# Start of a fused attention and feed-forward kernel: second weight chunk loaded behind the first tokens, one cast shared by two engines, one copy moved ahead, one more warming matmul

## The chip, the cores and the metric

The kernel runs on one core of a Trainium2 chip. The metric is the device time of one execution in microseconds (us). A core has five engines that run their own instruction streams in order and wait for each other by semaphores: TensorE (PE in the profile, with its weight loads as PEld), VectorE (DVE), ScalarE (ACT), GpSimd (POOL) and SyncE (SP). SP and ACT here also issue transfers between the chip's memory and the core's own memory.

## The reference, cut to what matters

Two branches read the same tokens x, 2048 of them with 512 channels, in 32-bit floats. Branch A is a sliding, dilated local attention with 32 heads of 16 channels and a window of 8 keys at a distance of 2. Branch B is a gated feed-forward layer with 1792 hidden channels. A sigmoid gate per token mixes both.

```
qkv = x @ wqkv                      # 512 -> 1536, split into q, k, v of 32 heads
logits = q . k[pos - 2*w], w = 0..7, scaled; softmax over w
a = (sum over w of attn * v[pos - 2*w]) @ wo
b = (gelu(x @ w_gate) * (x @ w_up)) @ w_down
g = sigmoid((x * gate_w).sum(-1))
out = g * a + (1 - g) * b
```

## The kernel before, in words

Every product of 32-bit matrices is made of three matmuls. An operand is split into a high part (rounded to the matmul's own format, `hi`, a copy on ACT) and a low part (the rest, `lo`, a subtraction on DVE). Then high times high, low times high and high times low are summed in a bank of the accumulator memory. The tokens come in two halves of 1024, and each half in 8 tiles of 128 tokens. The larger products are moreover done with a scheme of seven block products instead of eight, so that sums of blocks (s1, s2, t1 and so on) are formed first.

The change is only in the first microseconds, in `start()` (lines 867 to 1082), which makes the queries and keys of the first half of the tokens. What it holds:

- The weights of this stage are four blocks of 1024 columns, b11, b21, b12 and b22, each with two chunks k=0 and k=1 of 512 columns. The tokens are blocks a11, a12, a21 and a22, each with two chunks k=0 and k=1, of 128 channels by 512 tokens.
- Lines 72 to 80 run `WARM` matmuls on zeros, so that TensorE is at work while the first data is on its way.
- Lines 884 to 895 issue the loads. The two chunks of b11 (256 KB each) are issued by ACT (`nc.scalar`). SP issues the first 128 tokens of a11 k=0 (64 KB), its other 384 tokens (192 KB), a11 k=1 (256 KB), b21 (512 KB), then a12 and the rest.
- Lines 915 to 922 split the first operands: `tokens(0, P)` casts and subtracts the first 128 tokens on DVE, `hi("b11", 0)` is on ACT, `lo("b11", 0)` on DVE, then the other tokens, and the k=1 chunks of a11 and b11.
- Lines 923 to 933 are the matmuls of k=0: three for the first tile of 128 tokens, `FILLERS` (2) small ones on zeros, then nine for the other three tiles (t=1 to 3). Line 935 runs the twelve of k=1, tile by tile, three for each. That ends the first sums, U[0] to U[3].
- Lines 936 to 938 split b21 and a12 (the third chunk of weights and its tokens). Lines 939 to 941 copy the four sums U to four other banks V_ on ACT, and line 942 adds a12 times b21 to the copies, 24 matmuls, six for each tile: three with k=0, three with k=1.

What sets the order: `row`, `act` and `mms` (lines 775 to 789) are wrappers of DVE, ACT and PE that chain each instruction to the one written before it on that engine. So on these engines the order in time is the order in the program, and an instruction that waits holds back all that is written after it. In the profile all these instructions have line 787, so they are told apart by their tiles: `g<-prod` is a part of b11 or b21 (raw weights lie in `prod`), `A<-raw` a part of the tokens, `acc` the banks U, `p` the banks V_, `p<-acc` the copies of the sums.

After `start()` come the feed-forward products of the first half with the attention's vector work between them, then the same for the second half, and the output product.

Of the kernel before, what the change touches and what calls it, by code (L numbers as in the profile page):

```python
# [12 lines left out]
AF = mybir.ActivationFunctionType  # L13
# [16 lines left out]
UC = 128  # L30
UH = UC // DH
NU = D // UC
WARM = 16
FILLERS = 2
ASK = (0.3, 0.3, 0.3, 0.6, 1.0, 1.2, 1.2)
BEHIND = 150
# [2 lines left out]
BT = 4  # L39
# [5 lines left out]
QW = 2 * P  # L45
# [3 lines left out]
def tile_gated_mix(ctx: ExitStack, tc: tile.TileContext, xt, wqkv, wff, wo, out):  # L49
    nc = tc.nc  # L50
# [10 lines left out]
    def tl(tag, dt=F32):  # L61
        return pool.tile([P, COLS.get(tag, 512)], dt, name=tag, bufs=BUFS[tag])
# [5 lines left out]
    def bank(tag):  # L68
        return psum.tile([P, 512], F32, name=tag, bufs=BUFS.get(tag, 1))
# [6 lines left out]
    idle = [bank("p") for _ in range(4)]  # L76
    for i in range(WARM):
        c = i // 4 % 2 * QW
# [69 lines left out]
    def shift(par, queue, i, j):  # L148
        k = KQ["a"][:, :2 * NP - 1]
        if not i:  # L150
            nc.gpsimd.memset(k[:1, :NP - 1], 0.0)
        for a, b in (1, P - 15), (P - 15, P):
            queue.dma_start(k[a:b, i:j], k[a - 1:b - 1, NP + i:NP + j])
# [300 lines left out]
    def product(ps, a, w, start):  # L454
        for kc in range(2):
            ah, al = XOP[a, kc]
            wh, wl = (x[:, kc * P:(kc + 1) * P] for x in w)
            for n, (w_, a_) in enumerate(((wh, ah), (wh, al), (wl, ah))):
                LAST[:] = [nc.tensor.matmul(ps, w_, a_, start=(start and kc == 0 and n == 0),  # L459
                                            stop=(kc == 1 and n == 2), skip_group_check=True)]  # L460
# [328 lines left out]
    row, act, mms = Row(nc.vector), Row(nc.scalar), Row(nc.tensor)  # L789
# [5 lines left out]
    SRC, OP_, Q2, RAWS = {}, {}, {}, {}  # L795
# [15 lines left out]
    def hi(n, k):  # L811
        return act.activation(OP_[n, k][0], SRC[n, k], AF.Copy)

    def lo(n, k):
        h, l = OP_[n, k]
        row.tensor_tensor(l, SRC[n, k], h.bitcast(F32), op=OP.subtract)

    def both(f, *ns):
        for n in ns:
            for k in range(2):  # L820
                f(n, k)

    def sub(o, a, b):
        row.tensor_tensor(o, a, b, op=OP.subtract)
# [4 lines left out]
    def block(ps, a, w, first, kcs=(0, 1), ask=0.0):  # L829
        for t in range(BT):  # L830
            for kc in kcs:
                ah, al = OP_[a, kc]
                wh, wl = OP_[w, kc]
                for n, (a_, w_) in enumerate(((ah, wh), (al, wh), (ah, wl))):
                    mm(ps[t], t, a_, w_, first and kc == 0 and n == 0, kc == 1 and n == 2)
            if ask:
                pull(ask)

    def out_of(o, ps):
        act.activation(o, ps, AF.Copy)  # L840
# [26 lines left out]
    def start():  # L867
        room_x(0)
        wr = stage("prod", (2, W, UC))
        b11, b21 = wr[:, :1024], wr[:, 1024:]  # L870
# [6 lines left out]
        def load_w(dst, hh, half, cols=slice(0, 1024), queue=nc.sync):  # L877
            queue.dma_start(dst[:, cols], wqkv[hh, half, :, cols])

        def load_x(blk, kc, a=0, n=512):  # L880
            o = (2 * blk + kc // 2) * 512 + a
            nc.sync.dma_start(XR[kc % 2][:, o:o + n], xt[blk, :, kc, a:a + n])

        for k in range(2):
            load_w(b11, 0, 0, slice(k * 512, k * 512 + 512), nc.scalar)
        load_x(0, 0, 0, P)
        load_x(0, 0, P, 512 - P)
        load_x(0, 1)
        load_w(b21, 0, 1)
        load_x(0, 2)  # L890
# [16 lines left out]
        U = [bank(f"acc{t}") for t in range(BT)]  # L907

        def tokens(a, b):
            h, l = (x[:, a:b] for x in OP_["a11", 0])  # L910
            raw = SRC["a11", 0][:, a:b]
            row.tensor_copy(h, raw)
            row.tensor_tensor(l, raw, h.bitcast(F32), op=OP.subtract)

        tokens(0, P)
        hi("b11", 0)
        lo("b11", 0)
        tokens(P, 512)
        hi("a11", 1)
        hi("b11", 1)  # L920
        lo("a11", 1)
        lo("b11", 1)
        (xh, xl), (wh, wl) = OP_["a11", 0], OP_["b11", 0]
        mm(U[0], 0, xh, wh, True)
        mm(U[0], 0, xl, wh)
# [7 lines left out]
                mm(U[t], t, a, w)  # L933

        block(U, "a11", "b11", False, (1,))
        for n, k in (("b21", 0), ("a12", 0), ("b21", 1), ("a12", 1)):
            hi(n, k)
            lo(n, k)
        V_ = [bank("p") for _ in range(BT)]
        for t in range(BT):  # L940
            act.activation(V_[t], U[t], AF.Copy)
        block(V_, "a12", "b21", False)

        def put(jj, ps):
            take_first(0, ps, jj, lambda o, i: act.activation(o, i, AF.Copy))
# [22 lines left out]
        for k in range(2):  # L968
            row.tensor_tensor(s12[k], q[k][2], q[k][3], op=OP.add)
        put(0, V_[0])  # L970
        both(hi, "s1")
        put(1, V_[1])
        sub(b11, b12, b11)
        for k in range(2):
            hi("t1", k)
            lo("s1", k)
            lo("t1", k)
        put(2, V_[2])
        put(3, V_[3])
        shift(0, nc.sync, 0, BT - 1)  # L980
# [49 lines left out]
        for kc in range(KC):  # L1030
            t = tl("d", F32R)
# [89 lines left out]
    def kq_second():  # L1121
# [94 lines left out]
        done.add((1, 2))  # L1216

    start()
    gc = pool.tile([P, 2, NP], F32, name="gc")
    en = pool.tile([P, NP], F32, name="en")  # L1220
# [51 lines left out]
```

## Time and profile before

| | us |
|---|---|
| median of 3 runs | 597.06 (596.82 to 597.29) |
| the profiled execution's own time | 596.87 |
| its span, first to last instruction | 594.8 |
| PE busy | 590.1 |
| DVE busy | 529.4 |
| ACT busy | 389.9 |

A timeline row reads: start in us from the beginning of the span, duration, engine, line, operation, tiles written and read, shape, count, and in brackets the idle time of the engine before it with what ended it. A matmul's record is longer than its distance from the next, because matmuls are pipelined; the distance between starts is what counts. A row of the table by stretch has the stretch, its length, the busy time of PE, PEld, DVE, ACT and POOL, and then the granted clock, the share of busy DMA engines and their rate. An execution's time stands above its span by what lies around it, 2.07 us here.

### The profile page before, as it was taken

Reading aid. Unit: us, or ns where it says so; the run is one execution under the profiler, and the core shown is the slowest. Engines: PE = TensorE matmul, PEld = TensorE weight load, DVE = VectorE, ACT = ScalarE, POOL = GpSimd, SP = SyncE. Lnnn points to the kernel's source line nnn. Section 1 sums busy time; section 2 is a strip of 40 time slices with the busy share of each in tenths; the row PEclk is TensorE's granted clock in tenths of the full one; section 3 lists DMA queues with packets and bytes.
Section 4 is the critical chain, followed back from the end, with each engine's and each line's share of the span. In section 5 each row is a group of like instructions: output and inputs, shape, how many; then the busy total and the mean of one; then the engine's idle time right before and its main releaser. Section 6 shows DMA issues by size and latency. Waiting matters only on the chain.

```text
span 594.8 us, 8195 instructions
## 1 busy us (share of the span) xinstructions
PE 590.1 (99%) x2778; PEld 494.1 (83%) x2778; DVE 529.4 (89%) x618; ACT 389.9 (66%) x668; POOL 89.2 (15%) x121
## 2 busy tenths in 40 slices
PE   9999999999999999999999999999999999999997
PEld 6889988888888888888889988888888888888886
DVE  5997979899998999799989888999999989799952
ACT  5845556787679767788773375677668666885532
POOL 0501001111111111102035000111111111101300
PEclk9999999999999999999999999999999999999999
DMA  8789897988989898998589948795967796737924
GB/s 316 264 250 244 238 306 217 261 245 200 273 215 300 225 261 230 240 312 304 192 249 306 276 137 264 168 244 145 272 157 226 183 269 157 220 109 193 143 57 155
DMA packets 80449, 134.18 MB, mean 226 GB/s; under 512 B 8092, under 2 KB 46362, under 8 KB 80152
## 3 DMA queue, kind: packets, MB, share of 16 engines
q1 hardware_dynamic: 62890, 97.67, 49.9%
q0 software_dynamic: 12576, 32.97, 28.4%
q10 hardware_dynamic: 4942, 3.01, 1.6%
q8 instruction: 22, 0.36, 0.3%
q14 instruction: 19, 0.16, 0.1%
HBM read 68.30 MB, written 38.86 MB: 180 GB/s over the span
## 4 chain that ended last, share of the span: by engine, by line
PE 99%; DVE 0%; ACT 0%; issue 0%
PE p L459 45%; PE acc L502 13%; PE p L502 13%; PE acc L130 8%; PE acc L787 8%; PE p L720 5%; PE p L787 5%; PE acc L720 2%; PE p L79 1%; DVE r L766 0%; ACT rt L768 0%; DVE zero L73 0%
## 5 line engine op out<-in xcount | busy, mean ns | idle before, releaser
L459 PE MATMUL p<-S,g 128*128 128x512 f32 x672 | 166.5, 389 | 0.0
L459 PEld LDWEIGHTS p<-S,g 128*128 128x128 f32 x672 | 125.7, 188 | 25.8
L459 PE MATMUL p<-A,g 128*128 128x512 f32 x504 | 126.7, 390 | 0.0
L459 PEld LDWEIGHTS p<-A,g 128*128 128x128 f32 x504 | 94.3, 188 | 19.6
L417 POOL DMA_DIRECT2D g<-raw x40 | 34.5, 862 | 280.3 <-ACT g L416 208.8
L228 DVE TENSOR_REDUCE lg<-prod 128x128 f32<-128x2048 f32 x32 | 72.9, 2279 | 0.1
L502 PE MATMUL p<-d,hh 128*128 128x512 f32 x224 | 68.5, 389 | 0.0
L502 PE MATMUL acc<-d,hh 128*128 128x512 f32 x224 | 58.1, 389 | 0.0
L287 DVE TENSOR_TENSOR prod<-kq,lg 128x2048 f32<-128x2048 f32 x24 | 54.7, 2279 | 0.9 <-PE p L459 0.5
L421 ACT ACTIVATE g<-raw 128x1024 fp32r<-128x1024 f32 (+1 forms) x40 | 39.5, 991 | 19.0 <-PE p L459 19.0
L502 PEld LDWEIGHTS acc<-d,hh 128*128 128x128 f32 x224 | 42.0, 188 | 8.7
L502 PEld LDWEIGHTS p<-d,hh 128*128 128x128 f32 x224 | 42.0, 188 | 8.7
L416 ACT ACTIVATE g<-raw 128x1024 fp32r<-128x1024 f32 (+1 forms) x40 | 39.5, 987 | 12.0 <-DVE raw L398 4.6
L469 DVE TENSOR_TENSOR c<-p,s 128x512 f32<-128x512 f32 x56 | 37.8, 682 | 6.8 <-PE p L459 6.0
L464 ACT ACTIVATE s<-p 128x512 f32<-128x512 f32 x56 | 33.2, 594 | 15.0 <-PE p L459 13.5
L476 DVE TENSOR_TENSOR hl<-c,hh 128x512 fp32r<-128x512 f32 x56 | 38.1, 680 | 5.5 <-ACT hh L475 5.5
L502 PE MATMUL p<-d,hl 128*128 128x512 f32 x112 | 42.8, 389 | 0.0
L475 ACT ACTIVATE hh<-c 128x512 fp32r<-128x512 f32 x56 | 35.1, 628 | 10.7 <-DVE c L473 10.6
L473 DVE TENSOR_TENSOR c<-c 128x512 f32<-128x512 f32 x56 | 38.2, 682 | 4.3 <-ACT c L570 4.1
L518 ACT ACTIVATE rt<-p 128x512 f32<-128x512 f32 x48 | 28.2, 595 | 20.1 <-PE p L502 20.1
L291 DVE TENSOR_TENSOR prod<-prod 128x1024 f32<-128x1024 f32 x32 | 39.0, 1218 | 0.2
L130 PE MATMUL acc<-d,A 128*128 128x256 f32 (+1 forms) x288 | 37.9, 281 | 0.0
(183 smaller groups left out, 982.0 us busy)
## 6 DMA issues: line engine op xcount, KB each, us to landing
g<-raw POOLq DMA_DIRECT2D x27, 512.0 KB, 6.6
raw<-wff SPq DMA_DIRECT2D x42, 256.0 KB, 3.7
ws<-g SPq DMA_DIRECT2D x14, 768.0 KB, 6.2
g<-ws SPq DMA_DIRECT2D x14, 768.0 KB, 5.4
r<-wff SPq DMA_DIRECT2D x28, 256.0 KB, 4.8
d<-r POOLq DMA_DIRECT2D x24, 256.0 KB, 6.4
g<-raw POOLq DMA_DIRECT2D x13, 384.0 KB, 6.4
os<-tb SPq DMA_DIRECT2D x64, 64.0 KB, 3.8
```

The source lines that it names most:

```text
L130: LAST[:] = [nc.tensor.matmul(ps[:, :cn], a[:, t], w[:, c0:c0 + cn], start=(kc == 0 and n == 0), stop=(kc == KC - 1 and n == 2))]
L228: nc.vector.tensor_reduce(two_of(lg, jj), prod.rearrange("p j w (h d) -> p (j w) h d", d=DH), axis=AX.X, op=OP.add)
L287: paced(nc.vector.tensor_tensor(prod.rearrange("p j w (h d) -> p (j w) h d", d=DH), spans(v, jj).rearrange("p j w (h d) -> p j w h d", d=D ...
L291: nc.vector.tensor_tensor(prod[:, :, :4], prod[:, :, :4], prod[:, :, 4:], op=OP.add)
L416: nc.scalar.activation(lo, raw, AF.Copy, scale=-1.0)
L421: ins = nc.scalar.activation(hi, raw, AF.Copy)
L459: LAST[:] = [nc.tensor.matmul(ps, w_, a_, start=(start and kc == 0 and n == 0), stop=(kc == 1 and n == 2), skip_group_check=True)]
L473: nc.vector.tensor_tensor(ge, ge, up, op=OP.mult)
L476: nc.vector.tensor_tensor(hl_, ge, hh_.bitcast(F32), op=OP.subtract)
L502: ins = nc.tensor.matmul(pp, a[:, ts], w, start=(i == 0 and n == 0 and gr == 0), stop=(i == 1 and n == 2), skip_group_check=True)
L720: ins = nc.tensor.matmul(pa, a, b, start=(first and n == 0), stop=(last and n == 2), skip_group_check=True)
L787: return lambda *args, **kw: self.add(getattr(self.eng, name)(*args, **kw))
```

## The change

The constant `WARM` goes from 16 to 17. The second chunk of b11 is no longer issued by ACT, but by SP, behind the two loads of a11 k=0 and ahead of a11 k=1. The high part of b11 k=0 is made in two halves of 256 columns (`QW`), the first by ACT, the second by DVE ahead of the low part. The k=1 chunk of b11 is split ahead of that of a11, on both engines. The banks V_ are taken earlier, and the copy of U[0] stands in ACT's order ahead of the splits of b21 and a12; the other three copies stay behind them. `out_of` is the same copy on ACT as was written out before.

```diff
-WARM = 16
+WARM = 17
...
-        for k in range(2):
-            load_w(b11, 0, 0, slice(k * 512, k * 512 + 512), nc.scalar)
+        load_w(b11, 0, 0, slice(0, 512), nc.scalar)
         load_x(0, 0, 0, P)
         load_x(0, 0, P, 512 - P)
+        load_w(b11, 0, 0, slice(512, 1024))
         load_x(0, 1)
         load_w(b21, 0, 1)
...
         tokens(0, P)
-        hi("b11", 0)
+        wh, wraw = OP_["b11", 0][0], SRC["b11", 0]
+        act.activation(wh[:, :QW], wraw[:, :QW], AF.Copy)
+        row.tensor_copy(wh[:, QW:], wraw[:, QW:])
         lo("b11", 0)
         tokens(P, 512)
+        hi("b11", 1)
         hi("a11", 1)
-        hi("b11", 1)
+        lo("b11", 1)
         lo("a11", 1)
-        lo("b11", 1)
...
         block(U, "a11", "b11", False, (1,))
-        for n, k in (("b21", 0), ("a12", 0), ("b21", 1), ("a12", 1)):
+        V_ = [bank("p") for _ in range(BT)]
+        for t, (n, k) in enumerate((("b21", 0), ("a12", 0), ("b21", 1), ("a12", 1))):
+            if not t:
+                out_of(V_[t], U[t])
             hi(n, k)
             lo(n, k)
-        V_ = [bank("p") for _ in range(BT)]
-        for t in range(BT):
-            act.activation(V_[t], U[t], AF.Copy)
+        for t in range(1, BT):
+            out_of(V_[t], U[t])
         block(V_, "a12", "b21", False)
```

## The prediction

> **What bounds the kernel now.** I read the page first, its busy line and its chain, and then a table of busy time by stretch, because a mean over 595 us says nothing of the ten microseconds that the change touches.
>
> ```profile
> span 594.8 us, 8195 instructions
> PE 590.1 (99%) x2778; PEld 494.1 (83%) x2778; DVE 529.4 (89%) x618; ACT 389.9 (66%) x668; POOL 89.2 (15%) x121
> PE 99%; DVE 0%; ACT 0%; issue 0%
> ...
> 13.40:40.00 26.60, 26.60 (x119) 22.05 (x118) 24.56 (x37) 19.59 (x40) 8.38 (x16) 1.00 0.82 265
> 40.00:560.00 520.00, 520.00 (x2476) 437.94 (x2475) 480.88 (x548) 351.25 (x596) 78.25 (x98) 1.00 0.83 229
> ```
>
> The chain that ended last is TensorE for 99%, and from 13.40 us to 560 us PE's busy time equals the stretch (first figure the length, second PE). So whatever PE has lost or won when it enters the long stream at about 13.4 us is carried to the end one for one; nothing later absorbs it. The whole question is at what time PE reaches one given matmul there. I take the first matmul of the second token block after the partial sums are copied (V block, t=1), which starts at 13.13. The timeline of PE, first merged and then single instructions from narrow stretches:
>
> ```profile
> 1.07 3.60 PE L79 MATMUL p<-zero 128*128 128x256 bf16 x16 [1.07 <-DVE zero L73]
> 4.67 1.65 PE L787 MATMUL acc<-g,A 128*128 128x512 f32 x3
> 5.26 0.63 PE L787 MATMUL acc<-g,A 128*128 128x512 f32 x1
> 5.69 0.63 PE L787 MATMUL acc<-g,A 128*128 128x512 f32 x1
> 6.12 0.44 PE L787 MATMUL acc<-zero 128*128 128x128 bf16 x2
> 6.49 5.44 PE L787 MATMUL acc<-g,A 128*128 128x512 f32 x21
> 8.71 0.63 PE L787 MATMUL acc<-g,A 128*128 128x512 f32 x2
> 9.37 0.50 PE L787 MATMUL acc<-g,A 128*128 128x512 f32 x1
> 9.71 0.40 PE L787 MATMUL acc<-g,A 128*128 128x512 f32 x1
> 11.77 5.60 PE L787 MATMUL p<-g,A 128*128 128x512 f32 x24
> 12.68 0.39 PE L787 MATMUL p<-g,A 128*128 128x512 f32 x1
> 12.90 0.39 PE L787 MATMUL p<-g,A 128*128 128x512 f32 x1
> 13.13 0.39 PE L787 MATMUL p<-g,A 128*128 128x512 f32 x1
> ```
>
> Read the starts. 24 matmuls of the V block take 5.60, so one follows another at (5.60 - 0.39) / 23 = 0.227 us. Before about 6.6 the clock is half of that: 5.26 to 5.69 is 0.43 for the same 512 columns, and 5.26 - 4.67 = 0.59 shows 0.16 more for a first weight load that nothing covered. The nine of k=0 run from 6.49 to 8.71. In k=1 the second starts at 8.71 + 0.63 - 0.39 = 8.95, the third only at 9.37, and the fourth 0.34 after that, 0.11 over the rhythm: a restart after a wait costs 0.11. From there it is dense to 13.13 and beyond. The two engines that feed it, ACT first, then DVE:
>
> ```profile
> 3.99 0.63 ACT L787 ACTIVATE g<-prod 128x512 fp32r<-128x512 f32 x1 [1.02 <-DMA prod<-wqkv]
> 7.36 0.63 ACT L787 ACTIVATE A<-raw 128x512 fp32r<-128x512 f32 x1 [2.74 <-DMA raw<-xt]
> 7.90 0.62 ACT L787 ACTIVATE g<-prod 128x512 fp32r<-128x512 f32 x1
> 8.61 0.63 ACT L787 ACTIVATE g<-prod 128x512 fp32r<-128x512 f32 x1
> 9.28 0.63 ACT L787 ACTIVATE A<-raw 128x512 fp32r<-128x512 f32 x1
> 9.82 0.62 ACT L787 ACTIVATE g<-prod 128x512 fp32r<-128x512 f32 x1
> 10.34 0.62 ACT L787 ACTIVATE A<-raw 128x512 fp32r<-128x512 f32 x1
> 10.86 2.04 ACT L787 ACTIVATE p<-acc 128x512 f32<-128x512 f32 x4
> 13.33 0.39 ACT L787 ACTIVATE kq<-p 128x256 f32<-128x256 f32 x1 [0.43 <-PE p L787]
> ```
>
> ```profile
> 3.72 0.23 DVE L787 CAST A<-raw 128x128 fp32r<-128x128 f32 x1 [2.63 <-DMA raw<-xt]
> 3.98 0.29 DVE L787 TENSOR_TENSOR A<-raw,A 128x128 fp32r<-128x128 f32 x1
> 4.65 0.69 DVE L787 TENSOR_TENSOR g<-prod,g 128x512 fp32r<-128x512 f32 x1 [0.38 <-ACT g L787]
> 6.08 0.36 DVE L787 CAST A<-raw 128x384 fp32r<-128x384 f32 x1 [0.73 <-DMA raw<-xt]
> 8.02 0.69 DVE L787 TENSOR_TENSOR A<-raw,A 128x512 fp32r<-128x512 f32 x1 [0.99 <-ACT A L787]
> 8.63 0.68 DVE L787 TENSOR_TENSOR g<-prod,g 128x512 fp32r<-128x512 f32 x1
> 9.27 0.69 DVE L787 TENSOR_TENSOR g<-prod,g 128x512 fp32r<-128x512 f32 x1
> 9.95 0.69 DVE L787 TENSOR_TENSOR A<-raw,A 128x512 fp32r<-128x512 f32 x1
> 10.55 0.69 DVE L787 TENSOR_TENSOR g<-prod,g 128x512 fp32r<-128x512 f32 x1
> 11.16 0.69 DVE L787 TENSOR_TENSOR A<-raw,A 128x512 fp32r<-128x512 f32 x1
> ```
>
> On ACT: 3.99 is the high part of b11 k=0; 7.36 that of the tokens a11 k=1, at the moment when its data lands; 7.90 of b11 k=1; 8.61 to 10.34 the four of b21 and a12 (the third chunk), and 10.86 the four copies of the sums. On DVE the low parts follow: 8.02 a11, 8.63 b11, then four from 9.27 to 11.16 + 0.69 = 11.85. The third matmul of k=1 waits at 9.37 for b11's low part (8.63 + 0.68 = 9.31).
>
> **Part by part.** *One more warming matmul.* The 16 stand 0.21 apart ((3.60 - 0.42) / 15, a single one's record being twice that), so the last leaves the array at about 4.46 and a 17th fills the empty stretch to 4.67. It delays nothing that was ready before 4.67.
>
> *b11's high part by two engines.* ACT's 256 columns: the 256-column row at 13.33 is 0.39, so 3.99 + 0.39 = 4.38. DVE's cast of the other 256 lies between 0.23 (128) and 0.36 (384): 0.29, after the tokens' low part (3.98 + 0.29 = 4.27), so 4.56. The first matmul's operands are there at about 4.6 against 4.62, under the 17th warming matmul; between nothing and the uncovered 0.16 of weight load can be won. I take 0.10: the two cold ones after it move too, the two fillers end near 6.27. The low part then stands at 4.56 + 0.69 = 5.25, ahead of its matmul at 5.6.
>
> *The second weight chunk behind the tokens.* The issue rows:
>
> ```profile
> 0.75 0.90 ACTq L878 DMA_DIRECT2D prod<-wqkv  x2
> 0.76 1.34 SPq L882 DMA_DIRECT2D raw<-xt  x3
> 2.14 0.43 SPq L878 DMA_DIRECT2D prod<-wqkv  x1
> ```
>
> ACT loses its second issue (ACT waits for data until 3.99 anyway: nothing). On SP it becomes the third issue, so a11 k=1, b21 and the four loads behind them are each issued some 0.45 later. The remaining 384 token columns, which landed at 6.08, no longer share the DMA engines with 256 KB of weights. They land between 6.08 (no sharing before) and 0.62 earlier, at 5.46: b21's 512 KB came 1.25 behind a11 (7.36 to 8.61), and 256 KB is half of it. Their cast and a semaphore add 0.41 (6.08 to 6.49). Anything up to 5.86 is hidden under PE's own 6.27, so k=0's second token group starts at 6.27 instead of 6.49: 0.22 won if so, 0 if nothing moves. I take 0.22, since most of that span of landings gives it, and k=0 ends at 8.49.
>
> For a11 k=1 (7.36) there are two bounds. The bytes ahead of it are the same, so 7.36; or the weights now stand in its queue where a second queue carried them beside it: later by the same 0.62, so 7.98. The first is the nearer, since the late issue (about 2.1 to 2.6) is still five microseconds ahead of landing: I take 7.45. [...]
>
> *The order of the splits.* b11 k=1's high part goes ahead of a11's, its low part too, and both can be done before the tokens land, since the weights now stand ahead of them in one queue. So the wait at 9.37 goes, and what is late next is the low part of a11: high part 7.45 to 8.08, low part 8.11 to 8.80, second matmul of k=1 at 8.85, third at 8.85 + 0.34 = 9.19, fourth 9.42 against 9.71. So far the change is 0.29 ahead. If a11 lands earlier, PE's own 8.49 + 0.23 = 8.72 binds.
>
> *The first sum copied ahead of the third chunk.* This is the part that I expect to decide. Before, ACT went on to b21's high part when it landed (8.61) and copied all four sums at the end (10.86), when they were long finished. Now the copy of U[0] stands first in ACT's hand-written order, and it must wait for the third matmul of k=1. From the row at 13.33: ACT took up a sum 0.04 after its last matmul's end (12.90 + 0.39 = 13.29). So the copy starts at 9.19 + 0.39 + 0.04 = 9.62, while b21 has been there for a microsecond. Four high parts queue behind it, at ACT's rhythm of 0.52 (9.82, 10.34, 10.86): b21 k=0 at 10.14, done 10.77; a12 at 10.66; b21 k=1 at 11.18; a12 k=1 at 11.70, done 12.32. DVE's four low parts wait for these: first at 10.80, then at its rhythm of 0.61 (9.95, 10.55, 11.16): 11.41, 12.02, 12.63, the last done at 13.32. Before it was 11.85.
>
> The V block needs that last low part for its fifth matmul. It stood at 12.68, with 0.83 to spare; now it starts at 13.36, and the sixth 0.34 later at 13.70 against 12.90. So t=1 starts at 13.93 against 13.13. The three other copies start at 12.22 and follow at about 0.5 each (2.04 for four), each ahead of its use (13.93 for the first, 1.36 more for each further one). What the copy's early place brings is nothing: at 11.47 PE would have found U[0] copied in the old order as well (10.86 + 0.58 = 11.44).
>
> **Sum.** +0.80 us at t=1, and with dense PE behind it at the end. The ACT and DVE rows after 13.4 move by the same 0.8 or less. The profiled execution took 596.87 with a span of 594.8 (2.07 around it): 596.87 + 0.80 = 597.67. The median of the three timed runs, 597.06, is 0.19 above it, so on that scale 597.86; I name **597.7**. As a formula the loss is 0.80 + (landing of a11 - 7.45): +1.33 at 7.98. At the early end PE binds at 8.72 and restarts without the 0.11, so +0.56.
>
> **The rivals.**
> - *The copy is free and the gain stays.* ACT would have to run b21's high part first, that is, the order in the program isn't that on the engine (the change does not do what it says), or U[0] would be done near 8.6. Then the 0.29 of k=1 remains: 596.6. Against it: the copy is written into one ordered row per engine, and k=0 alone keeps PE until 8.5. Chance 0.13.
> - *Slower by over 0.2%.* The tokens a11 k=1 land late because the weight chunk sits ahead of them in the same queue. Each microsecond of it is a microsecond at the end; at 7.98 the time is 598.2 on the profile's scale and 598.4 on the median's. It passes 0.2% (1.2 us) from a landing of about 7.85 to 8.0 on. For it: the issue rows, a queue in place of two. Against it: the same bytes. Chance 0.12.
> - *The clock.* The new waits in the V block (a few tenths before the second matmul, 0.7 before the fifth), or another start phase, leave TensorE at half speed for nine matmuls more, at 0.43 instead of 0.23 each: 1.8 us, 599.5. Against it: the wait of 0.2 at 9.37 cost no clock (9.71 and on run at 0.227). [...] Chance 0.04.
>
> **The numbers.** Forecast (a loss of 0.3 to 1.1 us, which is within the 0.2% that a measurement of this kernel can tell from no change): 0.71. Rivals 0.13, 0.12, 0.04. The first rival stays within 0.2% but for 0.02. Of the second and third I count 0.15 in all as slower by over 0.2%. So faster 0.02, same 0.83, slower 0.15. The range goes from 596.8, part of the way to the first rival, to 598.4, the late landing on the median's scale.
>
> **What would show it.** Right, if in the new profile an ACT copy p<-acc stands before the g<-prod of the third chunk, idle before it on PE; the first of these high parts starts near 10.1 instead of 8.6; the fifth V matmul waits for DVE near 13.3; and the fourth matmul of k=1 is ahead of 9.71. Wrong, if the third chunk's high parts still begin by 9, if the DMA rows bring a11 k=1 before 7 or after 8, or if PE has new gaps after 14 us.

## The result and the profile after

The changed kernel takes 598.34 us (median of 22 runs, 597.62 to 598.78) against 597.02 (22 runs, 596.60 to 599.55). The ratio is 1.0016, with a 95% interval of 1.0011 to 1.0022: a small loss, clear of the noise, at the border of 0.2% (the medians by themselves give 1.0022). The profiled execution took 598.14, with a span of 596.0. Some executions of several versions, the one before too, take 1 to 4 us more, which widens some intervals below; in the three of them that were profiled (copy_back 598.51, load_alone 598.44, tokens_act 599.28) t=1 of the V block is at most 0.42 late, so most of it is lost after the start (in tokens_act PE stands 0.96 before 84.85 and 1.05 before 91.64).

The page of the changed kernel, span, busy line and chain:

```profile
span 596.0 us, 8199 instructions
...
PE 590.1 (99%) x2779; PEld 493.8 (83%) x2779; DVE 529.7 (89%) x619; ACT 389.3 (65%) x668; POOL 89.2 (15%) x121
...
PE 97%; DMA 2%; DVE 0%; SPq 0%; ACT 0%; issue 0%; DVEq 0%
```

PE's busy time is the same 590.1, and the span is 1.2 longer, so PE stands still for 1.2 more. Landings of data now make 2% of the chain where PE alone had 99%. The timeline of PE shows where (the last row is from a narrow stretch):

```profile
4.53 1.00 PE L787 MATMUL acc<-g,A 128*128 128x512 f32 x3
...
6.01 2.33 PE L787 MATMUL acc<-g,A 128*128 128x512 f32 x9 [0.35 <-DVE A L787]
8.55 0.50 PE L787 MATMUL acc<-g,A 128*128 128x512 f32 x1 [0.21 <-ACT A L787]
9.28 2.77 PE L787 MATMUL acc<-g,A 128*128 128x512 f32 x11 [0.23 <-DVE A L787]
11.89 0.39 PE L787 MATMUL p<-g,A 128*128 128x512 f32 x1
12.55 0.98 PE L787 MATMUL p<-g,A 128*128 128x512 f32 x3 [0.26 <-DVE A L787]
13.75 1.43 PE L787 MATMUL p<-g,A 128*128 128x512 f32 x5 [0.23 <-DVE A L787]
...
14.32 0.39 PE L787 MATMUL p<-g,A 128*128 128x512 f32 x1
```

Read it against the rows of before. The nine matmuls of k=0 start at 6.01 instead of 6.49: a gain. The first matmul of k=1 then waits for a11's high part, the second (9.28) for its low part, the second of the V block (12.55) and the fifth (13.75) for low parts of the third chunk. The reference point of the prediction, t=1 of the V block, is at 14.32 against 13.13: +1.19, and the span is longer by the same 1.2. (The brackets show less than PE lost, because a matmul's record is longer than its distance from the next: 0.39 against 0.23.) ACT and DVE say why:

```profile
3.69 0.42 ACT L787 ACTIVATE g<-prod 128x256 fp32r<-128x256 f32 x1 [1.20 <-DMA prod<-wqkv]
6.31 0.63 ACT L787 ACTIVATE g<-prod 128x512 fp32r<-128x512 f32 x1 [2.20 <-DMA prod<-wqkv]
7.87 0.63 ACT L787 ACTIVATE A<-raw 128x512 fp32r<-128x512 f32 x1 [0.93 <-DMA raw<-xt]
10.05 0.58 ACT L787 ACTIVATE p<-acc 128x512 f32<-128x512 f32 x1 [1.55 <-PE acc L787]
10.54 0.62 ACT L787 ACTIVATE g<-prod 128x512 fp32r<-128x512 f32 x1
...
12.10 0.62 ACT L787 ACTIVATE A<-raw 128x512 fp32r<-128x512 f32 x1
12.62 1.55 ACT L787 ACTIVATE p<-acc 128x512 f32<-128x512 f32 x3
```

```profile
3.90 0.29 DVE L787 CAST g<-prod 128x256 fp32r<-128x256 f32 x1
...
5.60 0.36 DVE L787 CAST A<-raw 128x384 fp32r<-128x384 f32 x1 [0.61 <-DMA raw<-xt]
...
8.53 0.69 DVE L787 TENSOR_TENSOR A<-raw,A 128x512 fp32r<-128x512 f32 x1 [0.87 <-ACT A L787]
11.20 0.69 DVE L787 TENSOR_TENSOR g<-prod,g 128x512 fp32r<-128x512 f32 x1 [1.97 <-ACT g L787]
...
13.01 0.68 DVE L787 TENSOR_TENSOR A<-raw,A 128x512 fp32r<-128x512 f32 x1
```

ACT stands for 1.55 us before the copy at 10.05, because U[0] isn't summed, and the third chunk's first high part, at 8.61 before, is at 10.54. DVE idles 1.97 behind it, and its last low part is done at 13.69 (11.85 before). And a11 k=1 is taken up at its landing, at 7.87 instead of 7.36. The third chunk had long been there: SP's row shows its next issue held back 0.9 by b21's transfer, until 9.10 (before, the same row at 8.60 goes with ACT taking up b21 at 8.61).

```profile
9.10 0.33 SPq L878 DMA_DIRECT2D tb<-wqkv  x1
```

### The profile page after: what moved, and what is told of

Same layout as the page of the kernel before. It is cut to its first block, busy times and chain, and to the rows that moved or that the text cites. A ratio compares the mean times of both kernels' runs of the same rounds, so it can differ in the third digit from the quotient of the medians.

```text
span 596.0 us, 8199 instructions
## 1 busy us (share of the span) xinstructions
PE 590.1 (99%) x2779; PEld 493.8 (83%) x2779; DVE 529.7 (89%) x619; ACT 389.3 (65%) x668; POOL 89.2 (15%) x121
## 4 chain that ended last, share of the span: by engine, by line
PE 97%; DMA 2%; DVE 0%; SPq 0%; ACT 0%; issue 0%; DVEq 0%
PE p L459 45%; PE p L502 13%; PE acc L502 13%; PE acc L130 8%; PE acc L787 6%; PE p L720 5%; PE p L787 5%; PE acc L720 2%; DMA raw<-xt 1%; DMA prod<-wqkv 1%; SPq L882 0%; DVE A L787 0%; DVE r L766 0%; ACT rt L768 0%; DVEq L787 0%
```

## The experiments

Theory 1: the copy ahead of the third chunk costs the time. Theory 2: the late landing behind the moved load does. Theory 3: clock and phase of the start. Later, on the load itself, Q: one queue alone moves less; O: what counts is what stands ahead. All kernels are made from the two shown. The table gives, from one profiled execution each, when ACT takes up a11 k=1 and begins the third chunk, and t=1 of the V block; then the median over that of the kernel before on the same chip.

| kernel | a11 k=1 | third chunk | t=1 | median, us over before |
|---|---|---|---|---|
| before | 7.36 | 8.61 | 13.13 | 0 |
| after | 7.87 | 10.54 | 14.32 | +1.32 |
| copy_alone | 7.27 | 10.31 | 14.09 | +1.02 |
| load_back | 7.67 | 10.34 | 14.12 | +1.09 |
| copy_back | 7.95 | 9.19 | 13.55 | +0.52 |
| copy_mid | 7.86 | 9.11 | 13.37 | +0.58 |
| load_alone | 7.42 | 8.66 | 13.21 | +0.47 |
| copy_load_back | 7.17 | 8.39 | 12.76 | -0.10 |
| tokens_act | 7.42 | 8.14 | 12.88 | -0.17 |
| third_act | 8.53 | 9.07 | 13.94 | +0.80 |
| warm_alone | 7.92 | 9.14 | 13.69 | +0.19 |
| best_tokens | 6.26 | 8.10 | 12.62 | -0.51 |

Two more, which issue the second weight chunk late, are told below.

**The copy put back (copy_back).**

```diff
-V_ = [bank("p") for _ in range(BT)]
-for t, (n, k) in enumerate((("b21", 0), ("a12", 0), ("b21", 1), ("a12", 1))):
-    if not t:
-        out_of(V_[t], U[t])
+for n, k in (("b21", 0), ("a12", 0), ("b21", 1), ("a12", 1)):
     hi(n, k)
     lo(n, k)
-for t in range(1, BT):
-    out_of(V_[t], U[t])
+V_ = [bank("p") for _ in range(BT)]
+for t in range(BT):
+    act.activation(V_[t], U[t], AF.Copy)
```

> The changed kernel with its one copy of U[0] put back behind the four splits. Theory 1 (the copy holds ACT back until U[0] is summed, and the third chunk's splits queue behind it): the high parts of b21 and a12 start at the landing of b21 (near 9.1) instead of 10.5, the last low part is done near 12.3, the fifth V matmul waits for nothing, t=1 of the V block starts near 13.25 against 13.13 before, and the time is within 0.3 of the kernel before (about 597.1 on the scale of a median of 597.0). Theory 2 (the late landing of a11 k=1 and b21 behind the moved weight chunk is the cost, the copy is nearly free): the time stays 0.8 or more above the kernel before (597.8 to 598.3). Theory 3 (the difference is clock and start phase): no clear change from the changed kernel.

Measured 597.53 against 597.01 (ratio 1.0010, 1.0001 to 1.0019). ACT:

```profile
7.95 0.63 ACT L787 ACTIVATE A<-raw 128x512 fp32r<-128x512 f32 x1 [0.63 <-DMA raw<-xt]
9.19 0.63 ACT L787 ACTIVATE g<-prod 128x512 fp32r<-128x512 f32 x1 [0.62 <-DMA prod<-wqkv]
```

ACT begins the third chunk when it lands (the bracket names the transfer, not PE). Of the changed kernel's 1.32 that takes away 0.8. The rest stands, more than theory 1 expected (0.3): a11 and b21 land about 0.6 later than in the profile of before.

**The copy alone (copy_alone)**: the kernel before with only the last hunk of the diff.

> The kernel before with only the copy of U[0] ahead of the splits of b21 and a12. Theory 1: third matmul of k=1 at 9.37 with a record of 0.50, copy from 9.91, high parts of the third chunk from 10.43, last low part done near 13.6, t=1 of the V block near 14.2, so +1.0 to +1.1 us (about 598.1). Theory 2: b21 and a11 land as before, so the time is within 0.3 of before (597.0 to 597.3). Theory 3: no change.

Measured 598.03 against 597.01 (1.0020, 1.0011 to 1.0029). ACT, and PE from a narrow stretch:

```profile
9.82 0.58 ACT L787 ACTIVATE p<-acc 128x512 f32<-128x512 f32 x1 [1.40 <-PE acc L787]
10.31 0.62 ACT L787 ACTIVATE g<-prod 128x512 fp32r<-128x512 f32 x1
```

```profile
14.09 0.40 PE L787 MATMUL p<-g,A 128*128 128x512 f32 x1
```

With the loads untouched (a11 at 7.27), ACT stands 1.40 before the copy, and t=1 is at 14.09. Theory 1 holds to about a tenth; theory 2 had allowed 0.3.

**The load alone (load_alone)**: the kernel before with only the second chunk's issue moved.

```diff
-for k in range(2):
-    load_w(b11, 0, 0, slice(k * 512, k * 512 + 512), nc.scalar)
+load_w(b11, 0, 0, slice(0, 512), nc.scalar)
 load_x(0, 0, 0, P)
 load_x(0, 0, P, 512 - P)
+load_w(b11, 0, 0, slice(512, 1024))
```

> The kernel before with only the second weight chunk issued by SP behind the first tokens. All theories: a11 k=1 lands about 0.5 later (near 7.87 instead of 7.36). Theory 1: with the old order of splits that shifts the wait for b11's low part to about 9.9, the V block starts near 12.26 instead of 11.77 and has its low parts in time, so +0.5 us (597.5). Theory 2: +1.0 to +1.3 us (598.0 to 598.3). If the late landing in the changed kernel was chance and not the queue, +0.0.

Measured 597.48 against 597.01 (1.0013, 1.0003 to 1.0023). The median is what theory 1 gave, but the trace doesn't show theory 1's reason. In the profiled execution (598.44) a11 came at 7.42, 0.06 late, not 0.5, and t=1 at 13.21, 0.08 late. The rest of the 1.5 us by which its span is longer than before's was lost later, in part where PE waits twice for ACT:

```profile
266.40 0.73 PE L502 MATMUL p<-d,hh 128*128 128x512 f32 x2 [0.31 <-ACT p L496]
269.01 0.73 PE L502 MATMUL p<-d,hh 128*128 128x512 f32 x2 [0.26 <-ACT p L496]
```

Of the 11 times, five are at or below before's median and four are 1.4 to 2.1 us above it. So the 0.47 is the middle of a wide spread (596.88 to 599.14), and it isn't shown to be the price of the moved load.

**Both back (copy_load_back)**: only cast, order of splits and 17 warming matmuls stay.

> The changed kernel without the two suspects: the copy behind the splits and the second weight chunk on ACT's queue again; cast by two engines, order of splits and 17 warming matmuls stay. Theory 1: a11 k=1 lands near 7.36, the wait for b11's low part is gone, the V block starts near 11.49 (bound by the copy of U[0], which ends at 11.44) instead of 11.77: -0.28 us (596.75), the only version ahead of before. Theory 2: the same or no change. Theory 3: +1.2 as in the changed kernel, if the 17th matmul or the cast is to blame.

Measured 596.91 against 597.01 (0.9998, 0.9989 to 1.0007): no change that can be told. PE in the profile:

```profile
6.49 5.08 PE L787 MATMUL acc<-g,A 128*128 128x512 f32 x21 [0.94 <-DVE A L787]
11.40 3.56 PE L787 MATMUL p<-g,A 128*128 128x512 f32 x15
```

The 21 matmuls from k=0 through k=1 take 5.08 instead of 5.44 and the V block starts at 11.40 instead of 11.77, dense: there is no wait in k=1. That alone doesn't prove the order of the splits: a11 was taken up 0.19 earlier here, which in the old order, by the rows of before, would put the third matmul of k=1 at 9.18, against 9.13 by PE's rhythm here. The run load_back below settles it. The three edits that stay cost nothing, so theory 3 falls for them.

**The copy between the second and third split (copy_mid).**

```diff
 for t, (n, k) in enumerate((("b21", 0), ("a12", 0), ("b21", 1), ("a12", 1))):
-    if not t:
+    if t == 2:
-        out_of(V_[t], U[t])
+        out_of(V_[0], U[0])
```

> The changed kernel with the copy of U[0] moved from ahead of the four splits of the third chunk to between the second and the third. Theory 1 (the copy is dear only because it stands there before U[0] is summed): two high parts run while ACT would have waited, the copy then waits little or not at all, the last low part is done near 12.6, the fifth V matmul does not wait, and the time is that of the kernel with the copy put back (+0.5 us over before, 597.5). Rival (each copy ahead of a split costs its own 0.5 us there, wherever it stands): about 598.0.

Measured 597.44 against 596.86 by the medians (the interval, 0.9989 to 1.0010, is too wide to tell a loss). ACT:

```profile
9.75 0.63 ACT L787 ACTIVATE A<-raw 128x512 fp32r<-128x512 f32 x1
10.29 0.58 ACT L787 ACTIVATE p<-acc 128x512 f32<-128x512 f32 x1
10.81 0.61 ACT L787 ACTIVATE g<-prod 128x512 fp32r<-128x512 f32 x1
```

Here the copy has no bracket: U[0] was ready when ACT came to it. The time is that of copy_back (0.58 over before, 0.52 there). So the copy isn't dear, waiting in that place is.

**The load back, the copy kept (load_back)**: the changed kernel with the second chunk on ACT's queue.

> The changed kernel with only the second weight chunk issued by ACT again; the copy of U[0] stays ahead of the third chunk. If the later landing in the changed kernel comes from the moved load and each microsecond of it is passed on through the copy, as the prediction's formula has it: a11 k=1 lands near 7.2 to 7.4 (7.9 at the most, as one execution with the old loads has shown), t=1 of the V block near 13.7 to 13.9, and the median is 0.6 to 0.8 over before (597.6 to 597.8). If the moved load costs nothing and the landings differ by chance alone: the time of the changed kernel, +1.2 to +1.4 (598.2 to 598.4).

Measured 597.88 against 596.79 (1.0022, 1.0007 to 1.0037): between the two expectations. ACT, then PE:

```profile
7.67 0.63 ACT L787 ACTIVATE A<-raw 128x512 fp32r<-128x512 f32 x1 [0.49 <-DMA raw<-xt]
9.85 0.58 ACT L787 ACTIVATE p<-acc 128x512 f32<-128x512 f32 x1 [1.54 <-PE acc L787]
```

```profile
6.60 5.27 PE L787 MATMUL acc<-g,A 128*128 128x512 f32 x21 [1.00 <-DVE A L787]
11.71 0.40 PE L787 MATMUL p<-g,A 128*128 128x512 f32 x1
```

The prediction's formula, 0.80 + (7.67 - 7.45) = 1.02, meets this execution (t=1 at 14.12, +0.99) as it meets the changed kernel's (0.80 + 7.87 - 7.45 = 1.22; +1.19). But a11 came at 7.67 with the old loads. The PE rows show the worth of the order of the splits: a11 is taken up 0.31 later than before, and yet from the start of k=0's second group to the V block it is 5.11 us (6.60 to 11.71) against 5.28 (6.49 to 11.77).

**The warming matmul alone (warm_alone)**: the kernel before with `WARM = 17`.

> The kernel before with 17 warming matmuls instead of 16. Theories 1 and Q: nothing that was ready waits for the 17th, within 0.2 us of before. Theory 3 (the warming matmul moves the clock's change): the profile's clock rises at another place in every execution anyway, so again no change that shows in the median; a change of 0.5 us or more would speak for it.

Measured 597.18 against 596.99 (0.9996, 0.9984 to 1.0009): no change. Its profile is worth a row:

```profile
7.92 0.63 ACT L787 ACTIVATE A<-raw 128x512 fp32r<-128x512 f32 x1 [3.49 <-DMA raw<-xt]
```

The loads are those of before, and a11 lands at 7.92, later than in the changed kernel. One profile can't tell the moved load from an ordinary late execution; only medians can.

**A second queue in use (tokens_act, third_act)**: copy_back, with a11 k=1 (first) or b21 (second) issued by ACT. For the first, `load_x` takes a `queue` argument.

```diff
-load_x(0, 1)
+load_x(0, 1, queue=nc.scalar)      # tokens_act
-load_w(b21, 0, 1)
+load_w(b21, 0, 1, queue=nc.scalar) # third_act
```

> The kernel with the copy put back, and a11 k=1 issued by ACT instead of SP, so that the second weight chunk stays behind the first tokens in SP's queue while a second queue is at work. Theory Q (one queue alone moves less in these microseconds, so all that follows lands late): a11 k=1 lands by 7.4 and b21 by 8.6 as in the kernel before, bytes from 5 to 7 us back near 380 to 400 GB/s, time 596.8 to 597.1. Theory O (only what stands ahead in the queue counts): a11 k=1 lands early, b21 still near 9.1, time 597.1 to 597.5.

> The kernel with the copy put back, and b21 (512 KB) issued by ACT instead of SP; a11 k=1 stays in SP's queue behind the second weight chunk. Theory Q (two queues at work move more in these microseconds): bytes from 5 to 7 us near 380 to 420 GB/s, a11 k=1 lands by about 7.4 though the same bytes stand ahead of it in its queue, and b21 lands by 8.6; time 596.7 to 597.0. Theory O (the bytes ahead in the queue count, and b21 on another queue only takes its share): a11 k=1 lands at 7.9 or later; time 597.4 or more.

tokens_act: 596.69 against 596.86 (0.9992, 0.9978 to 1.0006), by the medians 0.7 below copy_back's place; ACT takes b11 first there, at 6.88, so 7.42 in the table isn't a11's landing. third_act: 597.79 against 596.99 (1.0008, 0.9997 to 1.0020). Busy time from 5 to 7 us, the last number GB/s; before, after, tokens_act, warm_alone, in this order:

```profile
5.00:7.00 2.00, 2.00 (x7) 1.10 (x7) 1.24 (x3) 0.00 (x0) 0.00 (x0) 1.00 1.02 389
```

```profile
5.00:7.00 2.00, 1.65 (x9) 1.16 (x8) 0.95 (x3) 0.63 (x1) 0.00 (x0) 1.00 0.90 297
```

```profile
5.00:7.00 2.00, 2.00 (x7) 1.16 (x7) 0.92 (x2) 0.12 (x1) 0.00 (x0) 1.00 1.07 424
```

```profile
5.00:7.00 2.00, 1.34 (x7) 0.71 (x7) 0.98 (x3) 0.00 (x0) 0.00 (x0) 1.00 0.97 352
```

With a second queue at work on a11, 424 GB/s move and the third chunk is there by 8.14: for Q. But third_act brings a11 only at 8.53, as O expected, by which b21 takes its share beside it. And warm_alone's 352 with two queues lies as low as copy_back's 345 with one. So what is shown is that splitting the loads over two queues can repair the start (t=1 at 12.88 in tokens_act, at 13.55 in copy_back); that one queue as such is slower isn't.

**A late issue (weights_late, best_late)**: both back as above, but ACT issues the second chunk after its half of the cast; best_late also has k=1 reordered and the copy after the third split.

```diff
 for k in range(2):
-    load_w(b11, 0, 0, slice(k * 512, k * 512 + 512), nc.scalar)
+    k or load_w(b11, 0, 0, slice(0, 512), nc.scalar)
...
 act.activation(wh[:, :QW], wraw[:, :QW], AF.Copy)
+load_w(b11, 0, 0, slice(512, 1024), act)
...
-block(U, "a11", "b11", False, (1,))     # best_late, from here
+(xh, xl), (wh, wl) = OP_["a11", 1], OP_["b11", 1]
+for t in range(BT):
+    mm(U[t], t, xh, wh)
+for t in range(BT):
+    mm(U[t], t, xh, wl)
+    mm(U[t], t, xl, wh, False, True)
```

> The version with copy and load back, but ACT issues the second weight chunk only after its half of the first cast (near 4.1 instead of 1.2). Theory Q: the 384 tokens land near 5.4 to 5.6, since nothing shares the engines with them after the first chunk, the two queues then run together, a11 k=1 lands near 7.4, and the time is 596.7 to 597.0. Theory O: the weights come in beside a11 k=1 and b21 and delay both as in the changed kernel: 597.3 to 597.6.

> A version made to win: weights as in the late issue by ACT, cast by two engines, order of splits as changed, matmuls of k=1 reordered (four high times high first, then for each tile high times low and low times high), copy of U[0] after the third split. If PE in these microseconds is bound by landings and by ACT's order, as theory 1 has it: V block from about 11.1 instead of 11.77 without later waits, -0.4 to -0.6 us (596.4 to 596.6). If the landing is late, as in theory O: 597.0 to 597.3.

Measured 603.30 against 596.86 (1.0091, 1.0071 to 1.0110) and 601.52 (1.0066, 1.0050 to 1.0082). Every expectation missed, by more than 4 us. weights_late, ACT, then PE, then three stretches:

```profile
3.99 0.36 ACTq L787 DMA_DIRECT2D prod<-wqkv  x1
...
10.76 0.63 ACT L787 ACTIVATE g<-prod 128x512 fp32r<-128x512 f32 x1 [6.36 <-DMA prod<-wqkv]
```

```profile
11.96 0.51 PE L787 MATMUL acc<-g,A 128*128 128x512 f32 x1 [3.45 <-ACT A L787]
```

```profile
8.40:11.90 3.50, 0.11 (x1) 0.00 (x0) 0.48 (x1) 1.14 (x3) 0.00 (x0) 1.00 1.05 386
12.94:16.35 3.41, 3.41 (x9) 2.64 (x10) 3.41 (x7) 2.12 (x5) 0.00 (x0) 0.50 1.00 419
16.40:19.80 3.40, 3.40 (x17) 2.80 (x16) 1.10 (x2) 2.42 (x6) 0.00 (x0) 1.00 0.08 31
```

The 256 KB were issued at 3.99 and landed at 10.76. In the view of the queues no packet of ACT's moves between 4.2 and 7.2, while 0.93 MB move on SP's; from 7.2 to 10.6 its 0.26 MB move beside 0.97 MB of SP's. PE stood 3.45 us, and behind that the granted clock is 0.50 in the stretch from 12.94 to 16.35 (the number ahead of the DMA share), with 9 matmuls in 3.41 us where the next stretch, at 1.00, has 17.

**A version from what was learnt (best_tokens)**: the load behind the first tokens, a11 k=1 on ACT's queue, old order of splits (a11 now lands first), copy of U[0] after the third split.

```diff
-load_x(0, 1)
+load_x(0, 1, queue=nc.scalar)
...
-    if not t:
-        out_of(V_[t], U[t])
+    if t == 3:
+        out_of(V_[0], U[0])
```

> A version made to win: second weight chunk behind the first tokens on SP as in the changed kernel, but a11 k=1 issued by ACT so that two queues work; cast by two engines; old order of the splits of k=1, since a11 then lands first; copy of U[0] after the third split of the third chunk, where U[0] is long summed. By theories 1 and Q: a11 k=1 lands near 6.3, b21 near 8.2, no wait in k=1, V block dense, t=1 of the V block between 12.4 and 12.8 against 13.13 before: -0.3 to -0.7 us (596.3 to 596.7 where before has 597.0). If it is not below before, the start is bound by something that neither theory names.

Measured 596.48 (596.21 to 597.20, 12 runs) against 596.99: 0.9985, 0.9975 to 0.9996, faster than both kernels. ACT, then PE:

```profile
6.26 0.63 ACT L787 ACTIVATE A<-raw 128x512 fp32r<-128x512 f32 x1 [2.15 <-DMA raw<-xt]
...
9.28 0.62 ACT L787 ACTIVATE g<-prod 128x512 fp32r<-128x512 f32 x1
9.80 0.58 ACT L787 ACTIVATE p<-acc 128x512 f32<-128x512 f32 x1
10.32 0.61 ACT L787 ACTIVATE A<-raw 128x512 fp32r<-128x512 f32 x1
```

```profile
6.36 5.06 PE L787 MATMUL acc<-g,A 128*128 128x512 f32 x21 [0.70 <-DVE A L787]
11.26 3.56 PE L787 MATMUL p<-g,A 128*128 128x512 f32 x15
```

The copy waits for nothing, and from 6.36 on PE is dense: t=1 at 12.62 instead of 13.13, the 0.51 of the medians.

## Why the prediction was right, and which term was off

- *What is lost at the start is carried to the end.* Right: t=1 +1.19, span +1.2.
- *Warming and cast.* Right in kind. The first matmul starts at 4.53; the three first take 1.00 instead of 1.65, because in this execution the second and third start 0.23 apart (4.90 and 5.13), where it was 0.43 before. That the clock is half at 0.43 was the forecast's reading of the distances; the granted clock of the table is 1.00 from 3 to 7 us in both profiles. k=0 resumes 0.48 earlier, not 0.22. Worth nothing in the end: the first of k=1 waits for a11 anyway, at 8.55 against 8.71.
- *The tokens* landed at 5.60, inside the bounds of 5.46 and 6.08.
- *The order of the splits* takes the wait out of k=1, as worked out (load_back: with a11 0.31 later than before, the V block starts 0.06 earlier).
- *The copy ahead of the third chunk decides.* Right, and shown four ways: alone it costs 1.02; taken back it returns 0.8; two splits later it costs nothing that these times can tell (0.58 over before, against 0.52 with the copy put back); with the old loads it still costs 1.09. The chain behind it came as written, from ACT's wait on PE to the fifth V matmul's wait on DVE (13.36 forecast for a landing of 7.45, 13.75 with the landing 0.42 later).
- *The landing of a11 k=1* is the term that was mis-sized: taken as 7.45, between 7.36 and 7.98, it was 7.87. By the formula that is the 0.42 between the forecast +0.80 and the 1.2 found. I had weighed the same bytes ahead above the change of queue. With the copy put back, the moved load costs 0.62 by the medians (copy_back less copy_load_back, on one chip: nine of the latter's 11 times are at or below 597.17, and one of the former's). Under the copy it is 0.23 (the changed kernel less load_back), but there the two intervals overlap widely, so that the moved load's share of the 1.3 is not settled; the 0.47 of load_alone can't be put down to the landing. If it is really less under the copy, I would argue that the copy already keeps the third chunk waiting past its landing (9.10 to 10.54), so that only a11's matters.
- *The size.* By the medians the loss is 1.32 where 0.71 was forecast. The time, 598.34, lies inside the range only because the range's end, 598.4, had been put at the slow rival's late landing. That the loss still counts as within 0.2% is luck: the ratio is 1.0016, the medians by themselves give 1.0022.
- *The rivals.* The copy was not free: the order in the program held on ACT, and the third chunk began at 10.54. The clock was not lost to the waits in the V block: behind each of them matmuls start 0.23 to 0.24 apart (12.89 and 13.13, 14.09 and 14.32), and the granted clock is 1.00 from 11.89 to 15.00; the nine matmuls at half speed were an estimate that no run with such waits shows. The slow rival's landing (7.85 and later) was met in the profile, and the time came out at the border of 0.2% as it had it, with the mechanism of the forecast.

The 0.62 of copy_back over copy_load_back speaks for a landing that the moved load made later, though the edit changes the order of the loads as well as their queue. The single traces, a11 taken up at 7.17 to 7.92 with the old loads and 7.42 to 7.95 with only b11's first chunk left to ACT, don't settle it.

What stays open: why the same loads land up to 0.7 us apart between executions, and how much of 297 against 389 GB/s is the queue and how much the execution.

## What to carry to other kernels

On an engine that runs in order, as ACT did here (third chunk from 10.54, with the copy put back from 9.19), an instruction that waits for another engine's result belongs behind all work whose data is there sooner; look in the trace at what stands behind the wait, not at the price of the instruction. A copy that had 0.58 of its own cost 1.0 by its place and nothing that could be told two places later. Where a start is bound by landings, compare medians of several executions: a single profile moved by as much as the effect (a11 k=1 at 7.17 to 7.92 with the old loads, 0.62 by the medians for the moved load, copy_back less copy_load_back). And before a median's shift is put down to an edit, look in the trace whether the time is lost where the edit is: of the 1.5 us by which load_alone's profiled execution was longer, 1.4 were lost after the start.

## What the runs showed of the hardware that was not expected

- In weights_late a transfer issued late on a second queue was not served ahead of the first queue's backlog: issued at 3.99, landed at 10.76, without a packet of its own between 4.2 and 7.2 (in best_late ACT stood 6.45 for it, up to 10.55). Why is not shown.
- TensorE comes to its full rhythm at a different place from one execution to the next: the first three matmuls on data, started at 4.53 behind the same 17 warming matmuls, took 1.00 us in the profile of the changed kernel and 1.63 in that of tokens_act, with a granted clock of 1.00 from 3 to 7 us in both.
- After an idle time of 3.45 in weights_late the granted clock was 0.50 in the stretch from 12.94 to 16.35 and 1.00 from 16.40 on to 19.80; after one of 4.11 in best_late it was 0.50 from 11.30 to 14.60 and 1.00 from 14.70 to 18.00.
